# Transposing q and k of the last two units by transfers, fp32 dummy products and new orders in a fused linear-attention and max-out kernel

## The chip, the core and the metric

The kernel runs on one core of one Trainium2 chip. Times are device microseconds of one execution; the number of a kernel is the median of its runs.

## What is computed

The first half is a gated linear attention with a recurrent state of 48 x 48 for each of 4 batches and 8 heads, over 768 steps; its output, laid out as 3072 rows of 384, goes through a max-out layer (no bias) and an output product.

```python
for t in range(S):                                    # S = 768, D = 48, B = 4, H = 8
    state = alpha[:, :, t, :, None] * state + einsum('bhd,bhe->bhde', k[:, :, t], v[:, :, t])
    y[:, :, t] = einsum('bhd,bhde->bhe', q[:, :, t], state)
x = y.transpose(0, 2, 1, 3).reshape(3072, 384)
out = maximum(x @ w1, x @ w2) @ w_out                 # w1, w2: 384 x 1024, w_out: 1024 x 384
```

All inputs and the output are fp32. The kernel's products are in fp16, with sums in fp32.

## The kernel before, in words

The work is cut into 12 **units** of 256 rows (two chunks of 128 steps of one batch): unit u is batch u % 4, chunk pair u // 4. The layer is rewritten as max(x w1, x w2) w_out = relu(x (w1 - w2)) w_out + x (w2 w_out), so that each unit needs one product `h` against w1 - w2, a relu `g`, and a product `o` that adds the relu's share (`f` parts) and x's own share (`x` part).

Every step is an operation with a short name, which the orders below use. The number is the unit; units 0 and 1 are cut into two halves (.0, .1) for many steps.

- **Attention, up to the products.** `lg`, `ra`, `em`, `ep`, `de` (ScalarE: logarithm of alpha and exponentials), `sg` (sum of two steps' logarithms), `cs` (TensorE, L479 and L481: running sums of the logarithms), `k0`, `q0`, `kn`, `qn` (k and q times the decay factors, L414; `kn` on GpSimd or VectorE, `qn` on VectorE).
- **Transposes.** `tpq`, `tpk` (TensorE, L507): 16 transpositions each put q and k of a unit with the head's 48 channels along partitions, into two banks of PSUM; two copies `qk` (ScalarE or VectorE, L417) bring them to the tile QK in SBUF.
- **Attention products.** `pp` (L533, k against q, reads QK), `pt` (mask, VectorE, L545 and L550), `kv` (L582, new state), `tm`, `dd`, `sb` (state with its decay), `y` (L642: 112 or 88 small products from pt, v, QK and the state), `xt` (copy to fp16).
- **Layer.** `h` (L672, 6 products of 256 columns), `g` (L677 or L678), `o` (L699: an `f` part is two products, an `x` part three), `oc` (copy), `st` (store, issued from ScalarE's queue).
- **Weights, once.** `wt` (L382: w2 transposed in fp32, four transpositions a group, six groups), `wtc`, `woc` (to fp16), `w12` (w1 - w2 on VectorE, L398, four pieces), `wq` (L404: w2 w_out, 24 products), `wqc`.
- **Loads.** `ld.*`, all on SyncE's queue (L345 for alpha, q, k and v of the units, L367 for weights), 59 of them.

The program is written out by hand tables. ORDERS names, for each engine, every operation in the order in which the engine gets it. `Plan.follow` walks these tables with a planned duration for each operation. From the planned starts it takes two things: which of the eight banks of PSUM an operation gets, and where TensorE has gaps in the first 45 us. `Plan.gaps` lists the gaps, and `fill` puts **dummy products** of a tile of zeros (`wsrc`) there, sized so that they fill the gap. They keep TensorE running; nothing reads their result. An engine's instructions run in the order in which they stand, so a dummy that takes longer than its gap holds up what stands behind it. In `fill`, a gap that begins before 1.5 us counts double time.

Of the kernel before, what the change touches and what calls it, by code (L numbers as in the profile page):

```python
# [196 lines left out]
cs0.0 cs1.1 cs1.0 tpk0.0 cs0.1 tpq0.0 tpk1.1 pp0.0 tpk1.0 tpq1.1 kv1 tpq1.0 wt.20 pp1.0 tpq0.1 tpk0.1 kv0 pp1.1  # L197
wt.21 pp0.1 wt.10 wq.20 wq.21 wt.00 wt.01 y1.0 y1.1 y0.0 y0.1 wq.00 wq.22 wq.01 wq.10 wq.02 wq.23 wq.03 wq.11
wq.12 wt.11 wq.13 wq.24 wq.04 h0.0 wq.25 wq.05 h1.0 o0.0.f0 o0.1.f0 wq.14 wq.15 h1.1 h0.1 h0.2 wq.06 wq.26 wq.27
wq.16 wq.17 wq.07 cs2 o1.1.f0 o1.1.f1 o0.0.f1 h1.2 o0.1.f1 o0.1.f2 h0.3 cs3 o0.0.f2 o1.1.f2 h1.3 o0.0.f3 tpq2  # L200
tpk2 o0.1.f3 o0.1.x0 o1.1.f3 pp2 kv2 o1.1.x0 o0.0.x0 o1.0.f0 o1.0.f1 o1.0.f2 o1.0.f3 kv3 tpk3 tpq3 y2 o1.0.x0
cs4 h2.3 h2.0 h2.2 pp3 cs5 h2.1 o2.1.x0 o2.0.x0 o2.0.f0 o2.1.f0 tpq4 tpk4 y3 o2.1.f1 o2.0.f1 o2.0.f2 o2.1.f2
o2.0.f3 pp4 o2.1.f3 h3.3 h3.1 h3.0 o3.0.x0 kv4 tpq5 tpk5 kv5 cs6 h3.2 o3.0.f0 o3.0.f1 o3.1.x0 y4 o3.1.f0 o3.1.f1
o3.0.f2 o3.1.f2 o3.1.f3 pp5 h4.2 cs7 h4.1 o3.0.f3 h4.0 tpk6 kv6 tpq6 y5 o4.0.x0 o4.1.x0 o4.1.f0 h4.3 h5.0
o4.0.f0 h5.1 o4.1.f1 o4.0.f1 o4.1.f2 o4.1.f3 tpq7 tpk7 pp6 o4.0.f2 o5.1.x0 cs8 o4.0.f3 h5.2 h5.3 o5.1.f0 o5.1.f1
y6 kv7 tpk8 tpq8 o5.1.f2 o5.0.x0 o5.1.f3 o5.0.f0 o5.0.f1 pp7 o5.0.f2 cs9 h6.3 o5.0.f3 h6.0 h6.2 y7 pp8 tpk9 tpq9
h6.1 h7.3 h7.2 h7.1 o6.0.x0 o6.0.f0 h7.0 kv8 kv9 pp9 o6.1.x0 cs11 o7.1.x0 o6.0.f1 o7.1.f0 o6.0.f2 o7.1.f1
o6.1.f0 o6.1.f1 o7.1.f2 o6.1.f2 o6.1.f3 o6.0.f3 o7.0.x0 o7.0.f0 o7.0.f1 cs10 y8 y9 o7.0.f2 o7.0.f3 h8.3 h8.1
o7.1.f3 h8.2 h8.0 tpq11 kv11 tpk10 tpq10 tpk11 o9.1.x0 h9.0 h9.1 o9.0.x0 h9.2 kv10 pp10 o9.1.f0 o9.0.f0 h9.3
o9.1.f1 o9.0.f1 o9.0.f2 o9.1.f2 o8.0.x0 pp11 o8.1.x0 o8.0.f0 o8.1.f0 o9.0.f3 o8.1.f1 o8.1.f2 o8.0.f1 o8.0.f2 y10  # L210
y11 o8.0.f3 o9.1.f3 h10.0 h10.1 o10.1.x0 o10.0.x0 o10.0.f0 h11.2 h11.1 o11.0.x0 h11.0 o10.1.f0 h10.3 o11.1.x0
# [10 lines left out]
w6.01 w6.00 xt5.1 xt5.0 ep7 lg9 g4.3 g5.0 ra8 g5.1 oc4.1 w6.11 qk7.0 em8 de8 st2 ep8 g5.2 g5.3 lg10 oc4.0 xt6.1
qk8.0 ra9 oc5.1 xt6.0 em9 g6.3 ep9 oc5.0 de9 g6.0 g6.2 w9.10 st3 xt7.0 vc8 qk9.1 g6.1 st4 g7.3 lg11 st5 vc10
g7.0 w9.11 ra10 em11 de11 ep11 w10.01 ra11 w10.11 em10 xt8.0 xt8.1 de10 ep10 oc7.0 xt9.1 g8.1 w11.00 xt9.0
w10.00 g8.2 st6 w11.11 st7 qk10.0 qk11.0 g9.0 g9.1 g9.2 g9.3 xt10.0 xt11.0 g11.2 st9 g10.2 oc8.0 g10.3 oc8.1 st8
oc10.0 oc10.1 st10 st11.0 oc11.1 st11.1 st11.2
# [3 lines left out]
q00.0 qn0.0 kn1.1 q01.1 dm0 q01.0 k01.0 k00.1 qn1.1 qn1.0 qn0.1 pt0.0.1 qk1.0.1 pt0.0.0 tm1.0 pt1.0.0 qk0.1.0  # L230
tm0.0 pt1.1.1 pt1.1.0 pt1.0.1 pt0.1.1 pt0.1.0 tm0.1 xt1.1 zw2 xt0.0 w12.0 tm1.1 w12.1 wtc.11 g1.0 w12.2 g0.2
g0.1 w12.3 sg3 q02 qn2 k02 kn2 dm3 g1.3 qk2.1 qn3 k03 w2.00 tm2.0 pt2.0 pt2.1 tm3.0 qk3.1 xt2.1 qk3.0 tm3.1 g2.3
tm2.1 qn4 pt3.1 pt3.0 g2.1 qk4.0 qk4.1 k05 sg6 pt4.0 qn5 pt4.1 tm4.0 qk5.1 tm5.0 tm4.1 sb5.1 w5.00 k06 tm5.1 qn6
sg7 dm6 pt5.0 pt5.1 tm6.0 g4.0 dm7 vc7 k07 qk6.0 qk6.1 qn7 sb6.1 w7.11 tm6.1 qk7.1 pt6.1 pt6.0 qn8 kn8 w7.01
tm7.0 qk8.1 k09 pt7.1 pt7.0 tm7.1 qn9 xt7.1 dm9 pt8.1 pt8.0 qk9.0 g7.2 g7.1 sg11 tm8.0 tm9.0 sb9.1 pt9.0 pt9.1
q011 k010 oc6.1 oc6.0 q010 w9.01 kn10 k011 w11.01 qn10 qn11 oc7.1 sb11.0 g8.0 tm11.0 qk11.1 g8.3 qk10.1 tm10.0
w11.10 pt10.0 pt10.1 sb10.1 w10.10 pt11.0 pt11.1 xt10.1 oc9.0 g10.0 xt11.1 g10.1 g11.1 oc9.1 g11.0 g11.3 oc11.0
oc11.2
# [509 lines left out]
def kernel(  # L748
# [63 lines left out]
    def fill(t0, t1, b):  # L812
# [4 lines left out]
        while left > 0.06:  # L817
            cols = min(512, int(2400 * left / slow) - 5)
            nc.tensor.matmul(env["PB"][b][:, 0:cols], lhsT=w[:, 0:128], rhs=w[:, 0:cols], start=True, stop=True)  # L819
# [38 lines left out]
```

## Time and profile before

| | before |
|---|---|
| median of 3 runs (lowest, highest) | 133.82 us (133.79, 133.96) |
| profiled execution | 133.79 us, span 132.1 us |
| TensorE busy in the span | 124.8 us (95%), 2061 products |
| VectorE, ScalarE, GpSimd busy | 103.3, 95.4, 64.4 us |
| dummy products | 28, 9.4 us busy |
| loads and stores | 28.63 MB |

PE is TensorE's products, PEld its weight loads, DVE VectorE, ACT ScalarE, POOL GpSimd, SP SyncE; a q behind the name is the engine's queue, where transfers are issued. A row of the timeline is the start, the length, engine, line, operation, output and inputs, and how many such instructions follow each other. The length runs from the first start to the last end, and a product's end lies about 0.2 us behind the start of the next, since products are pipelined. A row of groups has count, busy time, mean of one in ns, and the idle time before them with what ended it. A row of a stretch has, for each engine, its busy time and its count. In the page's first line a TensorE that is busy may still be held up inside a product.

### The profile page before, as it was taken

Reading aid. Unit: us, or ns where it says so; the run is one execution under the profiler, and the core shown is the slowest. Engines: PE = TensorE matmul, PEld = TensorE weight load, DVE = VectorE, ACT = ScalarE, POOL = GpSimd, SP = SyncE. Lnnn points to the kernel's source line nnn. Section 1 sums busy time; section 2 is a strip of 40 time slices with the busy share of each in tenths; the row PEclk is TensorE's granted clock in tenths of the full one; section 3 lists DMA queues with packets and bytes.
Section 4 is the critical chain, followed back from the end, with each engine's and each line's share of the span. In section 5 each row is a group of like instructions: output and inputs, shape, how many; then the busy total and the mean of one; then the engine's idle time right before and its main releaser. Section 6 shows DMA issues by size and latency. Waiting matters only on the chain.

```text
span 132.1 us, 4911 instructions
## 1 busy us (share of the span) xinstructions
PE 124.8 (95%) x2061; PEld 88.9 (67%) x2061; DVE 103.3 (78%) x186; ACT 95.4 (72%) x198; POOL 64.4 (49%) x104
## 2 busy tenths in 40 slices
PE   6988889999999999999999999999999999999970
PEld 2444667777667766867776767976688765778650
DVE  5469997869999996998699969989988599355040
ACT  3688889568899999998996997998288920301540
POOL 6025970052759999958579399655146200000000
PEclk9999999999999999999999999999999999999999
DMA  3999999999999999999999999560003300002144
GB/s 89 325 325 363 415 371 342 341 297 260 252 302 311 280 261 293 322 334 251 318 314 270 300 275 285 193 241 5 0 5 122 121 0 0 5 0 90 69 181 144
DMA packets 56486, 28.63 MB, mean 217 GB/s; under 512 B 50320, under 2 KB 56080, under 8 KB 56464
## 3 DMA queue, kind: packets, MB, share of 16 engines
q1 hardware_dynamic: 53040, 23.60, 63.0%
q10 hardware_dynamic: 3424, 4.72, 9.9%
q8 instruction: 16, 0.26, 0.7%
q14 instruction: 6, 0.05, 0.1%
HBM read 23.59 MB, written 4.72 MB: 214 GB/s over the span
## 4 chain that ended last, share of the span: by engine, by line
PE 68%; SPq 7%; DVE 7%; DMA 6%; issue 4%; POOL 4%; DVEq 0%; POOLq 0%
PE pb L699 28%; PE pb L672 20%; PE pb L642 7%; SPq L345 6%; DMA w2f<-in_moe_w_dram 6%; PE pb L533 4%; PE pb L582 3%; PE pb L507 3%; PE pb L404 2%; SPq L367 2%; POOL kn L414 1%; DVE gt L677 1%; PE pb L382 1%; PE pb L479 1%; DVE w L417 1%
## 5 line engine op out<-in xcount | busy, mean ns | idle before, releaser
L699 PE MATMUL pb<-wo,gt 128*128 128x384 f16 (+2 forms) x200 | 37.5, 320 | 0.0
L672 PE MATMUL pb<-xt,w 128*128 128x256 f16 x288 | 36.5, 273 | 0.0
L672 PEld LDWEIGHTS <-w 128*128 128x128 f16 x288 | 27.6, 98 | 5.7
L678 ACT ACTIVATE gt<-pb 128x512 f16<-128x512 f32 x32 | 18.4, 600 | 11.5 <-PE pb L672 11.0
L545 DVE TENSOR_TENSOR pt<-pb,mask 128x1024 f16<-128x1024 f32 x20 | 23.6, 1217 | 2.5 <-PE pb L533 2.5
L699 PEld LDWEIGHTS <-gt 128*128 128x128 f16 x200 | 18.2, 98 | 9.9
L677 DVE TENSOR_SCALAR gt<-pb 128x512 f16<-128x512 f32 x16 | 10.9, 685 | 9.2 <-PE pb L672 8.8
L699 PE MATMUL pb<-w2o,xt 128*128 128x384 f16 (+2 forms) x75 | 15.2, 320 | 0.0
L417 ACT CAST xt<-pb 128x384 f16<-128x384 f32 x18 | 10.1, 592 | 5.6 <-PE pb L642 5.6
L414 POOL TENSOR_TENSOR sb<-tm,dd 128x384 f16<-128x384 f32 x15 | 12.9, 858 | 1.2 <-DVE tm L614 1.0
L614 DVE TENSOR_TENSOR tm<-pb,sb 128x384 f32<-128x384 f32 x16 | 8.6, 550 | 3.8 <-PE pb L582 3.5
L417 ACT COPY qk<-pb 128x1024 f16<-128x1024 f16 (+1 forms) x13 | 10.3, 818 | 1.6 <-PE pb L507 1.4
L417 ACT COPY os<-pb 128x384 f32<-128x384 f32 (+1 forms) x18 | 8.5, 473 | 3.9 <-PE pb L699 2.8
L819 PE MATMUL pb<-wsrc 128*128 128x512 f16 (+6 forms) x28 | 9.4, 480 | 1.3 <-DVE wsrc L825 1.3
L642 PE MATMUL pb<-pt,w 128*32 128x128 f16 x384 | 10.0, 220 | 0.0
L414 POOL TENSOR_TENSOR kn<-kf,em 128x768 f16<-128x768 f32 (+1 forms) x5 | 7.5, 1498 | 5.0 <-DVE kf L414 3.3
L417 DVE COPY qk<-pb 128x1024 f16<-128x1024 f16 (+1 forms) x15 | 9.5, 646 | 0.3
L414 POOL TENSOR_TENSOR qf<-qf,ra 128x384 f32<-128x384 f32 (+1 forms) x5 | 5.2, 1045 | 8.8 <-ACT pb L486 5.6
L484 ACT ACTIVATE em<-pb 128x384 f32<-128x384 f32 (+1 forms) x14 | 6.2, 442 | 4.5 <-PE pb L481 3.6
L642 PE MATMUL pb<-qk,sb 128*32 128x128 f16 x240 | 9.4, 219 | 0.0
L642 PEld LDWEIGHTS <-w 128*32 128x32 f16 x384 | 8.4, 96 | 1.5 <-issue 0.7
L699 PEld LDWEIGHTS <-xt 128*128 128x128 f16 x75 | 6.7, 98 | 3.5
(103 smaller groups left out, 232.1 us busy)
## 6 DMA issues: line engine op xcount, KB each, us to landing
out_dram<-os ACTq DMA_DIRECT2D x11, 384.0 KB, 3.0
af<-in_alpha_dram SPq DMA_DIRECT2D x8, 384.0 KB, 5.8
kf<-in_k_dram SPq DMA_DIRECT2D x8, 384.0 KB, 4.8
qf<-in_q_dram SPq DMA_DIRECT2D x8, 384.0 KB, 5.2
vf<-in_v_dram SPq DMA_DIRECT2D x8, 384.0 KB, 5.7
w2f<-in_moe_w_dram SPq DMA_DIRECT2D x3, 512.0 KB, 5.7
wof<-in_moe_w_out_dram SPq DMA_DIRECT2D x4, 384.0 KB, 8.6
w1f<-in_moe_w_dram SPq DMA_DIRECT2D x4, 384.0 KB, 9.8
```

The source lines that it names most:

```text
L345: nc.sync.dma_start(out=V(T_)[n].rearrange("p h r d -> p h (r d)"), in_=V(src)[b, :, t0 : t0 + 256, :].rearrange("h (p r) d -> p h (r d)", ...
L414: return lambda: getattr(nc, e).tensor_mul(out=o(), in0=x(), in1=y())
L417: return lambda: nc.scalar.copy(out=o(), in_=i()) if e == "scalar" else getattr(nc, e).tensor_copy(out=o(), in_=i())
L484: add(f"em{nq}", "ACT", lambda p=p, h_=h_: nc.scalar.activation(out=V("EM")[lg][:, h_], in_=csv(p), func=ACTF.Exp, scale=-1.0), 0.05 + 0.3 ...
L545: f = lambda e=e: nc.vector.tensor_mul(out=V("PT")[pt][:, e].rearrange("p a j x -> p (a j) x"), in0=pair(pp[e][0]).rearrange("p n (j x) -> ...
L614: nc.vector.tensor_add(out=V("TM")[new], in0=kvv, in1=V("SB")[m4])
L642: nc.tensor.matmul(o, lhsT=l, rhs=r, start=(a, qd) not in seen, stop=i == len(todo[qd]) - 1, skip_group_check=True)
L672: nc.tensor.matmul(t[:, m, :], lhsT=V("w12")[:, ds, f * 128 : f * 128 + 128], rhs=V("XT")[x3][:, ds, :], start=(ds == 0), stop=(ds == ND - 1))
L677: gd = lambda g2=g2, v2=v2: nc.vector.tensor_relu(out=g2(), in_=v2())
L678: ga = lambda g2=g2, v2=v2: nc.scalar.activation(out=g2(), in_=v2(), func=ACTF.Relu)
L699: nc.tensor.matmul(b32(x, w), lhsT=l, rhs=r, start=fst and y_ == 0, stop=lst and y_ == len(ws) - 1)
L819: nc.tensor.matmul(env["PB"][b][:, 0:cols], lhsT=w[:, 0:128], rhs=w[:, 0:cols], start=True, stop=True)
```

## The change

Four things change.

1. **q and k of units 10 and 11** are not transposed on TensorE any more. Eight transposing transfers on SyncE's queue (two each for q and k of each unit, 64 partitions x 1024 fp16 each), behind all loads, go from the tiles KN and QN straight into QK. The 64 transpositions and the four copies `qk` of these units go.
2. For that, `kn` and `qn` of these two units are written in another layout, each by two instructions of half the size, and `kv` of these units reads KN in that layout.
3. **Dummy products** read an fp32 `wsrc` instead of an fp16 one. `fill` and `fills` now reckon 1200 columns a microsecond where they had 2400.
4. All five **orders** are new, the loads' order too: the w1 loads come ahead of the second half of w_out, and w2.0 and w2.1 are the first weights. With new planned starts the banks of PSUM and the gaps for dummies differ too.

```diff
-                    count += 2 * self.fills(t - pe - 0.25)
+                    count += 2 * self.fills((t - pe - 0.25) / (2 if pe == 1.2 else 1))
...
     def fills(left):
-        return int(left / 0.215) + (left % 0.215 > 0.06)
+        return int(left / 0.43) + (left % 0.43 > 0.06)
...
     "SP": """
-ld.af0 ld.af1 ld.kf0 ld.kf1 ld.qf0 ld.qf1 ld.vf1 ld.vf0 ld.w2.2 ld.wo.0 ld.w2.1 ld.w2.0 ld.wo.1 ld.wo.2 ld.w1.0
...
+ld.af1 ld.af0 ld.kf0 ld.qf0 ld.qf1 ld.vf1 ld.kf1 ld.vf0 ld.w2.0 ld.w2.1 ld.wo.0 ld.wo.1 ld.w2.2 ld.w1.0 ld.w1.1
...
+TURN = (10, 11)
...
+            def kq(e, nm, src, fac, h_=h_):
+                def f():
+                    eng = getattr(nc, e)
+                    if u not in TURN:
+                        eng.tensor_mul(out=V(nm)[i3][:, :, h_, 0:D], in0=rhd(src())[:, :, h_], in1=bc(fac()))
+                        return
+                    o = V(nm)[i3].rearrange("p r h w -> p (r h w)").rearrange("p (j r e w) -> p r j e w", j=HP, r=2, e=2)
+                    for r in range(2):
+                        pe_ = lambda t: t.rearrange("p (j e) d -> p j e d", e=2)
+                        eng.tensor_mul(out=o[:, r, :, :, 0:D], in0=pe_(src()[:, :, r]), in1=pe_(fac()))
+                return f
...
-            for w, nm in enumerate(("qn", "kn")):
+            for w, nm in enumerate(("qn", "kn")) if u in TURN else ():
+
+                for a in range(2):
+                    add(f"ld.t{nm[0]}{u}.{a}", "SP", lambda w=w, nm=nm.upper(), a=a: nc.sync.dma_start(
+                        out=V("QK")[qk][:, a, w].rearrange("p j r c -> p (j r) c"),
+                        in_=V(nm)[i3][64 * a : 64 * a + 64].rearrange("p r h w -> p (r h w)"), transpose=True),
+                        1.25, reads=both(nm, i3), writes=[("qk", (qk, a), w)], key=P.nload, lat=1.9)
+                    P.nload += 1
+            for w, nm in enumerate(("qn", "kn")) if u not in TURN else ():
...
-            for a in range(2):
+            for a in range(2) if u not in TURN else ():
...
-    sbt("wsrc", [128, 512], FP16)
+    sbt("wsrc", [128, 512], FP32)
...
-            cols = min(512, int(2400 * left / slow) - 5)
+            cols = min(512, int(1200 * left / slow) - 5)
             nc.tensor.matmul(env["PB"][b][:, 0:cols], lhsT=w[:, 0:128], rhs=w[:, 0:cols], start=True, stop=True)
-            left -= (cols / 2400 + 0.002) * slow
+            left -= (cols / 1200 + 0.002) * slow
```

Three places of the orders matter below. The first is the head of TensorE's program. Before, the first batch of dummies ends like this, ahead of the first `cs` (tri and sg are its operands):

```order
L819 LDWEIGHTS wsrc_150
L819 MATMUL pb<-wsrc_150 128x512
L819 LDWEIGHTS wsrc_150
L819 MATMUL pb<-wsrc_150 128x479
L479 LDWEIGHTS tri_148
L479 MATMUL pb<-sg_83,tri_148 128x192
```

Now the program begins with six fp32 dummies; an fp32 product has no weight load of its own in this list:

```order
L840 MATMUL pb<-wsrc_150 128x512 x5
L840 MATMUL pb<-wsrc_150 128x477
L480 LDWEIGHTS tri_148
L480 MATMUL pb<-sg_84,tri_148 128x192
L482 LDWEIGHTS sg_84
L482 MATMUL pb<-ind_149,sg_84 128x4
```

And between the last `cs` and the first transposition (L527) stand six more:

```order
L482 LDWEIGHTS sg_83
L482 MATMUL pb<-ind_149,sg_83 128x4
L840 MATMUL pb<-wsrc_150 128x512 x5
L840 MATMUL pb<-wsrc_150 128x242
L527 LDWEIGHTS kn_89
L527 MATMUL pb<-ident_145,kn_89 128x64
```

Before, dummies stood between the `cs` as well; now all four `cs` stand together, with the two batches around them. Two smaller batches follow, of 384 columns ahead of the first `pp` and of 512 + 449 columns behind the second.

The second place is the end of SyncE's program. Before, it ends with the loads of units 10 and 11 (wof is the tile of w_out, used again for a unit's loads):

```order
L345 DMA wof_64<-in_v_dram 128x8x96
L345 DMA vf_79<-in_v_dram 128x8x96
L345 DMA wof_64<-in_k_dram 128x8x96
L345 DMA vf_80<-in_v_dram 128x8x96
L345 DMA wof_64<-in_q_dram 128x8x96
L345 DMA kf_72<-in_k_dram 128x8x96
L345 DMA qf_76<-in_q_dram 128x8x96
```

Now the transfers stand behind the last loads; qk_127 belongs to unit 10, qk_128 to unit 11:

```order
L346 DMA vf_80<-in_v_dram 128x8x96
L346 DMA wof_64<-in_v_dram 128x8x96
L515 DMA_TRANSPOSE qk_127<-kn_90 128x8x64
L515 DMA_TRANSPOSE qk_127<-qn_93 128x8x64 x2
L515 DMA_TRANSPOSE qk_127<-kn_90 128x8x64
L515 DMA_TRANSPOSE qk_128<-qn_94 128x8x64
L515 DMA_TRANSPOSE qk_128<-kn_91 128x8x64 x2
L515 DMA_TRANSPOSE qk_128<-qn_94 128x8x64
```

Unit 10's four transfers are issued first, then unit 11's four, and nothing is behind them.

The third place is VectorE's program where it makes q and k of unit 10 (kn_90, qn_93) and q of unit 11 (qn_94), after unit 9's `pt` (pt_129). Before:

```order
L545 TENSOR_TENSOR pt_129<-pb,mask_147 128x1024 x2
L414 TENSOR_TENSOR wof_64<-wof_64,ra_86 128x8x48
L414 TENSOR_TENSOR kf_72<-kf_72,af_68 128x8x48
L417 COPY os_138<-pb 128x384 x2
L414 TENSOR_TENSOR qf_76<-qf_76,ra_85 128x8x48
L417 CAST w_95<-vf_79 64x8x48
L414 TENSOR_TENSOR kn_90<-kf_72,em_87 128x16x48
L414 TENSOR_TENSOR wof_64<-wof_64 128x8x48
L417 CAST w_97<-wof_64 64x8x48
L414 TENSOR_TENSOR qn_93<-qf_76,pb 128x16x48
L414 TENSOR_TENSOR qn_94<-wof_64,pb 128x16x48
```

Now:

```order
L565 TENSOR_TENSOR pt_129<-pb,mask_147 128x1024 x2
L415 TENSOR_TENSOR qf_76<-qf_76,ra_85 128x8x48
L502 TENSOR_TENSOR kn_90<-kf_72,em_87 128x4x2x48 x2
L502 TENSOR_TENSOR qn_93<-qf_76,pb 128x4x2x48 x2
L418 CAST vc_99<-vf_80 128x768
L588 TENSOR_TENSOR de_103<-ex_114,own_113 128x32
L418 COPY os_138<-pb 128x384
L415 TENSOR_TENSOR wof_64<-wof_64,ra_86 128x8x48
L418 CAST xt_132<-pb 128x3x2x64
L502 TENSOR_TENSOR qn_94<-wof_64,pb 128x4x2x48 x2
```

k and q of unit 10 now follow unit 9's `pt` almost at once, each in two halves, and q of unit 11 comes after five other instructions. On TensorE `kv10`, `pp10`, `y10`, then `kv11`, `pp11` and later `y11` stand where units 8, 9 and 10 still have `h` and `o` products to do between them.

More of the change, by code (lines that the diff above doesn't have):

```diff
@@ L196 @@
     "PE": """
[L197 to L211, printed above, removed]
@@ L212 @@
-h10.2 o11.0.f0 o10.0.f1 o11.0.f1 o8.1.f3 o10.1.f1 o10.1.f2 o10.0.f2 h11.3 o10.0.f3 o11.1.f0 o11.0.f2 o10.1.f3
-o11.0.f3 o11.1.f1 o11.1.f2 o11.1.f3 o11.2.x0 o11.2.f0 o11.2.f1 o11.2.f2 o11.2.f3
+cs1.1 cs1.0 cs0.0 cs0.1 tpk0.0 tpq0.1 tpk0.1 tpq0.0 pp0.1 pp0.0 tpq1.1 tpk1.1 wt.01 kv0 pp1.1 wt.00 wt.10 tpk1.0
+tpq1.0 kv1 wt.11 pp1.0 y0.0 y0.1 wq.00 wq.10 wt.20 wq.11 wq.12 wq.01 wq.02 wq.03 wq.20 wq.21 wq.22 y1.0 y1.1
+h0.0 wt.21 wq.23 h1.0 h0.1 h1.1 h0.2 o0.0.f0 wq.13 h1.2 cs2 wq.24 o0.1.f0 wq.25 wq.04 wq.14 o0.0.f1 wq.15
@@ new lines @@
+o4.0.f0 o4.1.f0 o4.1.f1 o4.0.f1 o4.0.f2 h5.0 o4.0.f3 h5.1 pp6 tpk7 tpq7 o4.1.f2 o4.1.f3 o5.0.x0 h5.2 h5.3 y6 kv7
+tpq8 tpk8 o5.0.f0 o5.1.x0 h6.3 o5.0.f1 o5.0.f2 o5.1.f0 pp7 cs9 o5.1.f1 o5.1.f2 h6.0 o5.1.f3 o5.0.f3 h6.2 y7 pp8
+tpk9 tpq9 h6.1 h7.0 h7.1 o6.0.x0 o6.0.f0 kv8 kv9 pp9 o6.0.f1 cs10 o6.0.f2 h7.3 o6.1.x0 o6.0.f3 o6.1.f0 o7.0.x0
+o7.0.f0 o6.1.f1 y8 y9 o6.1.f2 h7.2 cs11 o7.1.x0 o6.1.f3 o7.0.f1 o7.0.f2 o7.1.f0 o7.0.f3 o7.1.f1 o7.1.f2 h8.1
+h8.2 o7.1.f3 h8.0 h9.3 o8.0.x0 o8.0.f0 o8.0.f1 h8.3 o8.0.f2 o8.1.x0 o8.1.f0 kv10 pp10 o8.0.f3 h9.2 o8.1.f1 h9.1
@@ L222 @@
[L222 to L226, printed above, removed]
+lg1.1 lg1.0 lg0.1 lg0.0 ra1.1 ra0.1 em1.1 em1.0 ra0.0 em0.0 em0.1 de1.0 de0.1 de0.0 ep1.1 ep0.0 ep1.0 de1.1
@@ L230 @@
[L230 to L238, printed above, removed]
+ind zsb0 zw0 zw1 zw2 zkn0 zsb1 zkn1 zqn2 zsg0 zsb2 own zsg1 sg1.1 trj zqn0 sg1.0 sg0.1 sg0.0 q00.1 k00.1 zqn1
+kn0.1 kn0.0 qn0.1 qn0.0 qk0.1.0 qk0.0.0 k01.1 k01.0 pt0.1.0 qn1.1 pt0.0.0 qk1.1.1 qn1.0 pt0.0.1 tm0.0 pt1.1.0
@@ L239 @@
+kn10 qn10 vc10 dm10 oc6.1 q011 xt9.0 qn11 g8.2 w11.01 g8.1 sb10.0 g8.3 tm10.0 pt10.0 pt10.1 g9.1 oc8.0 xt10.0
+sb11.0 xt10.1 pt11.1 oc8.1 pt11.0 tm11.0 sb11.1 g10.0 w11.10 xt11.0 g11.1 g11.2 oc10.0 oc10.1 oc11.2
 """,
     "POOL": """
-id16 id32 mask tri q00.1 kn1.0 dm1 dd0.1 vc0 w0.00 kn0.1 dd1.1 zsb3 woc.1 zsb1 sb1.1 w1.01 sb0.1 w1.11 woc.7 sg2
-dm2 dd2.1 q03 dd3.1 vc2 kn3 sb2.1 w3.01 sg4 sb3.1 sg5 q04 k04 dm4 kn4 q05 dd4.1 dm5 dd4.0 w4.11 dd5.0 sb4.0 kn5
-q06 sb5.0 w5.10 dd5.1 sb4.1 w5.11 kn6 sg8 dd6.0 vc6 sb6.0 q07 kn7 dd6.1 dd7.0 q08 k08 dd7.1 w6.10 sb7.0 sg9 sg10
@@ new lines, in gla @@
+            emf = lambda h_=h_: V("EM")[lg][:, h_]
+            two = 0.06 if u in TURN else 0.0
+            add(f"kn{nq}", "POOL", kq("gpsimd", "KN", KFn, emf), 0.2 + 1.6 / cut + 3 * two,
+                sh=True, reads=tk("kf", n, p) + tk("em", lg, p), writes=tk("kn", i3, p), key=q1("kn"),
+                alts={"DVE": (kq("vector", "KN", KFn, emf), 0.06 + 0.815 / cut + two)})
+            add(f"qn{nq}", "DVE", kq("vector", "QN", QFn, lambda p=p: csv(p)),
+                0.07 + 0.8 / cut + two, reads=tk("qf", n, p) + tk("csx", u, p) + [("dex", u, p)], writes=tk("qn", i3, p), ps=[cs[p]], key=q1("kn"))
```

55 lines of the change are left out of this document (35 added, 20 removed).

## Prediction

> **What bounds the kernel now.** I read the page first, then TensorE's busy time in stretches of the span, then TensorE's waits, then the chain that ended last, and at the end the timeline of the first 24 us. From the page, the stretches and the waits of TensorE from 19 us on:
>
> ```profile
> PE 124.8 (95%) x2061; PEld 88.9 (67%) x2061; DVE 103.3 (78%) x186; ACT 95.4 (72%) x198; POOL 64.4 (49%) x104
> 23.86:128.10 104.24, 104.04 (x1768) 76.71 (x1766) 84.55 (x125) 76.58 (x153) 53.65 (x75) 1.00 0.68 194
> PE pb L382 <- DMA w2f<-in_moe_w_dram: 0.4, 1, 0.4
> ```
>
> From 23.86 us, where the first `h` product (h0.0) starts, TensorE is busy in 104.04 of 104.24 us, and its only listed wait after 19 us is 0.4 us for a weight load. VectorE (84.55) and ScalarE (76.58) have room in the same stretch. So the end is the start of h0.0 plus the products that are then left. The chain, then the timeline of TensorE:
>
> ```profile
> 11.11 7.76 DMA w2f<-in_moe_w_dram
> 21.53 1.57 PE pb L404 x9
> 26.63 1.98 PE pb L672 x18
> 125.26 2.80 PE pb L699 x27
> 1.25 4.85 PE L819 MATMUL pb<-wsrc 128*128 128x512 f16 x11 [1.25 <-DVE wsrc L825]
> 5.89 0.37 PE L479 MATMUL pb<-sg,tri 128*128 128x192 f16 x1
> 6.15 0.88 PE L819 MATMUL pb<-wsrc 128*128 128x512 f16 x2
> 7.22 0.97 PE L819 MATMUL pb<-wsrc 128*128 128x512 f16 x4
> 23.86 0.82 PE L672 MATMUL pb<-xt,w 128*128 128x256 f16 x6
> ```
>
> The dummies (L819) fill the start. Products stop at 128.06 us; the last copy and store behind them are not touched. So there are two questions: how much product work the change takes from those 104.2 us, and when h0.0 can start.
>
> **The work left at h0.0.** The rows for what leaves and for what moves across h0.0:
>
> ```profile
> 34.60 0.41 PE L507 MATMUL pb<-ident,qn 64*128 64x64 f16 x16
> 34.84 0.40 PE L507 MATMUL pb<-ident,kn 64*128 64x64 f16 x16
> L382 PE MATMUL pb<-ident,w2f x24: 272/273/330, 14.1 to 23.3; 128*128 128x128 f32 x24
> 19.00 1.06 PE L382 MATMUL pb<-ident,w2f 128*128 128x128 f32 x8 [0.44 <-DMA w2f<-in_moe_w_dram]
> ```
>
> A group of 16 transpositions takes 0.24 us (34.60 to 34.84). Four groups go (tpq and tpk of units 10 and 11): 0.96 us. I add 0.1 us for one turn fewer between kinds of product in the new list: 1.05 us less in all. But the new list has done less when it comes to h0.0: 10 `wq` products instead of 14 (1.57 over 9, 0.17 each) and 5 groups of `wt` instead of 6 (eight transpositions of w2f in 1.06 us, less the last one's own 0.27, over seven: 0.11 each, 0.45 a group of four). That puts 1.1 us back. So about 104.3 us are left at h0.0 in both kernels, and the difference in time is the difference in h0.0's start. The four copies `qk` out of PSUM that go too (two on ScalarE, two on VectorE) were beside TensorE's work: nothing.
>
> **The dummies.** In fp16 and warm a column costs 1.98 us over 18 x 256, 0.43 ns. At the start it is twice that: the first eleven dummies hold 10 x 512 + 479 = 5599 columns and take 4.64 us (1.25 to 5.89), 0.83 ns. The rate changes between the dummies of 6.15 and those of 7.22 us; I take 7.1. In fp32 the trace has only the transpositions of w2f, 0.11 us for 128 columns: 0.86 ns, twice fp16. That is one pass. The built program holds one weight load and one product for each of those, but two of each for every fp32 dummy; a plain fp32 product is not in the trace. So a dummy's column costs between 0.86 ns (if both passes together cost what this one does) and 1.72 ns (if each does). I take 1.72, since the two are the same kind of instruction as the measured one. `fill` sizes them at 1200 columns a us, 0.83 ns: by my value each batch runs twice as long as its gap.
>
> The Trainium skill's FP8 and Floating Point Precision page (TensorE Precision Notes) says that a true fp32 product takes four passes through the array; four times 0.43 would be 1.72 ns too, and no run here shows it yet.
>
> The memset ahead of the first batch:
>
> ```profile
> 0.92 0.27 DVE L825 MEMSET wsrc<- 128x256 uint32 x1 [0.92 <-PEq L842]
> ```
>
> The new list has 15 dummies in four batches: 5 x 512 + 477 = 3037 columns ahead of cs1.1; 5 x 512 + 242 = 2802 ahead of tpk0.0; 384; 961. The first starts at 1.5 us (1.25, and 0.27 more for twice the words). Up to 7.1 us it gets through 5.6 / 0.00344 = 1630 columns, the other 1407 take 2.4 us: end at 9.5, where the old `cs` stood at 5.89. Four `cs` halves, 0.13 us each (half of 5.89 to 6.15): 10.05. The second batch, 2802 x 1.72 ns = 4.8 us: 14.85. Meanwhile ScalarE and VectorE need, from 10.05 on, by these rows:
>
> ```profile
> L484 ACT ACTIVATE em<-pb 128x192 f32<-128x192 f32 x4 | 1.3, 323 | 0.3 <-PE pb L481 0.3
> L486 ACT ACTIVATE pb<-pb 128x192 f32<-128x192 f32 x4 | 1.3, 331 | 0.0
> L488 ACT ACTIVATE ex<-pb 128x8 f32<-128x8 f32 x4 | 0.7, 172 | 0.3 <-PE pb L481 0.3
> L464 ACT ACTIVATE ra<-lg 128x192 f32<-128x192 f16 x4 | 1.4, 348 | 0.0
> L414 DVE TENSOR_TENSOR qn<-qf,pb 128x384 f16<-128x384 f32 x4 | 2.0, 547 | 0.1
> ```
>
> 1.3 + 1.3 + 0.7, one of the fourth (0.35) and one `qn` (0.5): 14.2. So kn and qn are ready before the dummies let the transpositions through. These, four halves of 0.12 and a turn, end at 15.4.
>
> **From there to h0.0.** VectorE's list from the first transpositions to w12.0, which h0.0 reads, has these beside `qn`:
>
> ```profile
> L550 DVE TENSOR_TENSOR pt<-pb,mask 128x512 f16<-128x512 f32 x8 | 5.1, 682 | 0.0
> L417 DVE COPY qk<-pb 128x512 f16<-128x512 f16 x2 | 0.8, 418 | 0.1
> L414 DVE TENSOR_TENSOR kf<-kf,af 128x192 f32<-128x192 f32 x4 | 1.3, 352 | 0.2 <-DMA kf<-in_k_dram 0.2
> L616 DVE COPY tm<-pb 128x384 f32<-128x384 f32 x4 | 2.2, 548 | 0.0
> L398 DVE TENSOR_TENSOR w<-w1f,w2f 128x768 f16<-128x768 f32 x4 | 3.8, 950 | 0.2 <-DMA w1f<-in_moe_w_dram 0.2
> 22.27 0.96 DVE L398 TENSOR_TENSOR w<-w1f,w2f 128x768 f16<-128x768 f32 x1 [0.15 <-DMA w1f<-in_moe_w_dram]
> ```
>
> Eight pt 5.1, four qk 1.6, two qn 1.0, two kf 0.65, two tm 1.1, one small memset 0.15 (half of 0.27), one w12 0.95: 10.6 us. So w12.0 ends at 26.0 and h0.0 starts at 26.1. TensorE's own items there (the last two batches, 2.3 us; wt 2.2; wq 1.7; the small products of units 0 and 1) fit beside it. In before, w12.0 waited for its load (last row) and h0.0 stood at 23.86. The new load order brings w1.0 one load sooner, but after this delay nothing waits for a load, so that gain is covered. h0.0 is 2.25 us later, the end 2.3: 134.4 us of span. The profiled execution took 133.79 us with a span of 132.1 (the median is 133.82), so 136.1.
>
> **The transposing transfers.** They replace products, if they land in time. Rows for what TensorE has to do meanwhile, for VectorE, and for the bounds:
>
> ```profile
> 78.71 0.55 PE pb L533 x16
> 79.69 0.16 PE pb L479
> 79.86 0.08 PE pb L481 x4
> 90.42 4.90 PE pb L699 x30
> 95.56 1.68 PE pb L642 x112
> L545 DVE TENSOR_TENSOR pt<-pb,mask 128x1024 f16<-128x1024 f32 x20 | 23.6, 1217 | 2.5 <-PE pb L533 2.5
> L414 DVE TENSOR_TENSOR kn<-kf,em 128x384 f16<-128x384 f32 x2 | 1.1, 553 | 0.0
> 10.12 0.43 SPq L367 DMA_DIRECT2D wof<-in_moe_w_out_dram  x1
> 17.32 4.26 SPq L367 DMA_DIRECT2D wof<-in_moe_w_out_dram  x1
> 79.02 1.39 SPq L345 DMA_DIRECT2D qf<-in_q_dram  x1
> out_dram<-os ACTq DMA_DIRECT2D x1, 128.0 KB, 2.0
> ```
>
> After pp9 VectorE has two pt (2.35), q0 (0.55, as large as half a kn), kn10 and qn10 in two halves each (2.2): the first transfer can go 5.1 us after pp9. The loads are then over (last issue 79.02) and nothing else is queued on SP. From pp9 to kv10 TensorE has pp9 (0.55), two cs (0.5), 53 products of `o` (4.90 over 30: 8.7), seven `h` (0.66 each: 4.6) and two `y` (1.7): 16 us; and 4.5 more to pp11. With t from one issue to the next and 2.0 us from issue to landing (the 128 KB store, the same size), pp10 waits if 5.1 + 4t + 2 is over 16, pp11 if 5.1 + 8t + 2 is over 20.5: from t = 1.7. The rows bound t between 0.43 and 4.26; I take 1.4, the last ordinary load's issue: no wait. The halves of kn and qn cost VectorE a few tenths, beside TensorE.
>
> **Rivals.** One: *the fp32 dummies take what `fill` plans* (0.86 ns). Then the first batch ends at 6.7 and the second before 10; 3.65 us of ScalarE and one qn after `cs` (7.25) give the transpositions at 11.4, and VectorE's 10.6 us from 11.8 give w12.0 at 22.3, when w1.0 has landed too. h0.0 at 22.4, 1.45 us sooner than before: 132.4. Against it speaks the pass of 0.11 us; for it, that the fp32 weight load may be what holds that row, and that columns alone cost less. Chance 0.16.
>
> Two: *the transfers are late*. The price is 8 us for each us of t above 1.7: at 3 us, 10 us more, near 146. For it, the 4.26 us issue; against it, that this one was issued while the loads ahead of it filled the queue. Chance 0.06. The Trainium skill's VectorE: DVE Perf Modes page (The three transpose paths) gives 1309 ns for 128x128 by DMA; as an estimate from that page, the four such areas of one transfer, one after the other, make t 5.2 us and the end 28 us later. No run here shows it.
>
> The forecast (two passes a dummy, transfers in time) has 0.78.
>
> **Numbers.** The forecast is 136.1. If the clock comes 2 us sooner, the first batch ends 1 us sooner, and the durations summed above overlap at their ends by up to 1 us in all: 134.0. If VectorE waits for ScalarE's qk copies (1 us) and the new order has waits of its own (0.9 us): 138.0. That holds the forecast's 0.78 and a little of the late transfers. The three runs of before spread by 0.13%, so 0.2% is about what can be told from no change. Faster 0.16 (rival one), same 0.02 (the foot of the forecast), slower 0.82.
>
> **What would show it.** In the profile after: two rows of products for each dummy, a warm pass of 512 columns near 0.44 us; `cs` from 9.5 us; the first transpositions at 15; h0.0 at 26; TensorE dense after it; pp10 and pp11 without a wait for a DMA. The prediction is wrong if h0.0 starts before 24 us, or if pp10 or pp11 waits for the transfers.

## The result, and the profile after

The changed kernel takes 135.58 us (median of 4 runs, 135.12 to 136.34) against 133.82 us (133.79 to 133.96): a ratio of 1.0135, 95% interval 1.0087 to 1.0183. The profiled execution took 135.12 us with a span of 133.4 us. Further down, the ratios leave out executions that are over 1.5% slower than their kernel's fastest (the medians do not), and the profiled executions with the second batch halved, with the late batches halved and with the transpositions placed anew are among these, so only the places of single steps are read from them.

Busy time and the group of the dummies on the page:

```profile
PE 128.4 (96%) x1999; PEld 90.5 (68%) x1999; DVE 101.0 (76%) x185; ACT 91.2 (68%) x189; POOL 67.9 (51%) x114
L840 PE MATMUL pb<-wsrc 128*128 128x512 f32 (+4 forms) x30 | 14.9, 644 | 1.5 <-DVE ind L300 1.5
```

TensorE has 62 products fewer and is busy 3.6 us longer. The 15 dummies are 30 rows of products, two for each, 14.9 us against 9.4 before. The stretch from the first `h` product to the last product:

```profile
26.29:130.02 103.73, 103.71 (x1715) 76.57 (x1711) 82.83 (x127) 73.52 (x147) 56.08 (x83) 1.00 0.74 199
```

From h0.0 on TensorE is dense, as before. Its timeline up to there, and its last row:

```profile
1.52 7.18 PE L840 MATMUL pb<-wsrc 128*128 128x512 f32 x12 [1.52 <-DVE ind L300]
8.53 0.25 PE L480 MATMUL pb<-sg,tri 128*128 128x192 f16 x1
9.07 4.95 PE L840 MATMUL pb<-wsrc 128*128 128x512 f32 x12
13.95 0.29 PE L527 MATMUL pb<-ident,kn 64*128 64x64 f16 x8
26.29 0.83 PE L693 MATMUL pb<-xt,w 128*128 128x256 f16 x6
129.39 0.61 PE L720 MATMUL pb<-wo,gt 128*128 128x128 f16 x8
```

The first `cs` (L480) stands at 8.53 where it stood at 5.89, the first transposition (L527) at 13.95, h0.0 at 26.29 where it stood at 23.86. From h0.0 to the last product's end it is 103.71 us (26.29 to 130.00), before 104.20. The transfers, by their source line:

```profile
L515 SPq DMA_TRANSPOSE qk<-kn x4: 1221/1263/1287, 96.4 to 105.0; - x4
L515 SPq DMA_TRANSPOSE qk<-qn x4: 1200/1242/1814, 97.8 to 106.3; - x4
DMA to landing us min/median/max: 2.6/2.7/3.8
107.02 0.23 PE L553 MATMUL pb<-qk 48*128 48x128 f16 x1
111.85 0.23 PE L553 MATMUL pb<-qk 48*128 48x128 f16 x1
```

Eight issues from 96.4 to 106.3 us are 1.41 us from one to the next. Unit 10's last transfer lands at 103.7, and pp10, its reader, starts at 107.02; unit 11's last lands at 109.0 (106.3 and 2.7), and pp11 starts at 111.85. TensorE's list of waits has one row, the start:

```profile
PE pb L840 <- DVE ind L300: 1.5, 1, 1.5
```

### The profile page after: what moved, and what is told of

It reads as the page before. It is cut to its first block, busy times and chain, and to the rows that moved or that the text cites. A ratio compares the mean times of both kernels' runs of the same rounds, so it can differ in the third digit from the quotient of the medians.

```text
span 133.4 us, 4799 instructions
## 1 busy us (share of the span) xinstructions
PE 128.4 (96%) x1999; PEld 90.5 (68%) x1999; DVE 101.0 (76%) x185; ACT 91.2 (68%) x189; POOL 67.9 (51%) x114
## 4 chain that ended last, share of the span: by engine, by line
PE 93%; DVE 3%; issue 1%; ACT 0%; ACTq 0%
PE pb L720 32%; PE pb L693 24%; PE pb L840 11%; PE pb L663 8%; PE pb L553 5%; PE pb L527 4%; PE pb L405 3%; PE pb L602 3%; PE pb L480 2%; DVE pt L570 1%; PE pb L383 1%; PE pb L482 1%; DVE tm L637 0%; ACT os L418 0%; DVE wsrc L846 0%
## 5 line engine op out<-in xcount | busy, mean ns | idle before, releaser
L720 PE MATMUL pb<-wo,gt 128*128 128x384 f16 (+2 forms) x200 | 39.3, 320 | 0.0
L698 DVE TENSOR_SCALAR gt<-pb 128x512 f16<-128x512 f32 x17 | 11.6, 686 | 7.9 <-PE pb L693 7.8
L840 PE MATMUL pb<-wsrc 128*128 128x512 f32 (+4 forms) x30 | 14.9, 644 | 1.5 <-DVE ind L300 1.5
L418 DVE COPY qk<-pb 128x1024 f16<-128x1024 f16 (+1 forms) x14 | 8.4, 608 | 4.2 <-PE pb L527 4.2
L840 PEld LDWEIGHTS pb<-wsrc 128*128 128x128 f32 x30 | 6.1, 214 | 8.0 <-issue 6.4
L418 ACT COPY qk<-pb 128x1024 f16<-128x1024 f16 (+1 forms) x10 | 8.4, 846 | 3.4 <-PE pb L527 3.4
L663 PE MATMUL pb<-pt,w 128*32 128x128 f16 x384 | 10.4, 220 | 0.0
L663 PEld LDWEIGHTS <-w 128*32 128x32 f16 x384 | 8.5, 96 | 2.7 <-issue 2.0
L418 ACT CAST w<-vf 64x384 f16<-64x384 f32 x19 | 9.7, 509 | 0.3
L418 ACT COPY os<-pb 128x384 f32<-128x384 f32 (+1 forms) x15 | 7.1, 470 | 4.0 <-DVE os L418 2.7
L663 PE MATMUL pb<-qk,sb 128*32 128x128 f16 x240 | 9.7, 219 | 0.0
```

The costliest lines, as they stand in the source:

```text
L418: return lambda: nc.scalar.copy(out=o(), in_=i()) if e == "scalar" else getattr(nc, e).tensor_copy(out=o(), in_=i())
L663: nc.tensor.matmul(o, lhsT=l, rhs=r, start=(a, qd) not in seen, stop=i == len(todo[qd]) - 1, skip_group_check=True)
L698: gd = lambda g2=g2, v2=v2: nc.vector.tensor_relu(out=g2(), in_=v2())
L720: nc.tensor.matmul(b32(x, w), lhsT=l, rhs=r, start=fst and y_ == 0, stop=lst and y_ == len(ws) - 1)
```

## The experiments

The theory: the fp32 dummies take twice the time that `fill` plans for them, that puts h0.0 later, and transfers and orders cost nothing. The rivals: the new orders or the transfers cost the time; the type itself does harm; or the transfers are worth nothing. All ratios are against the kernel before on the same chip.

| kernel | median us | ratio to before (95%) | first cs | first transposition | h0.0 |
|---|---|---|---|---|---|
| changed | 135.58 | 1.0135 (1.0087, 1.0183) | 8.53 | 13.95 | 26.29 |
| changed, fp16 dummies | 132.39 | 0.9869 (0.9832, 0.9905) | 5.50 | 10.62 | 23.09 |
| changed, half the fp32 columns | 132.33 | 0.9882 (0.9843, 0.9921) | 6.04 | 10.71 | 23.18 |
| changed, no dummies | 132.94 | 0.9903 (0.9868, 0.9938) | 5.63 | 10.30 | 24.49 |
| before, fp32 dummies | 137.79 | 1.0265 (1.0224, 1.0306) | 8.82 | 11.83 | 28.21 |
| changed, first batch halved | 134.61 | 1.0057 (1.0037, 1.0076) | 6.36 | 11.83 | 25.20 |
| changed, second batch halved | 134.59 | 1.0036 (1.0011, 1.0062) | 9.50 | 12.57 | 26.54 |
| changed, late batches halved | 134.85 | 1.0065 (1.0028, 1.0102) | 9.53 | 14.94 | 26.59 |
| fp16 dummies, transpositions back | 135.25 | 1.0061 (1.0034, 1.0087) | 6.14 | 10.53 | 23.48 |
| the same, placed anew | 134.10 | 1.0000 (0.9974, 1.0025) | 6.02 | 10.68 | 23.68 |
| before, transfers alone | 134.76 | 1.0055 (1.0039, 1.0072) | 5.89 | 7.76 | 24.41 |
| changed, each transfer twice | 152.24 | 1.1375 (1.1354, 1.1397) | 8.47 | 13.88 | 26.23 |

**The dummies' type.** In the changed kernel:

```diff
-    sbt("wsrc", [128, 512], FP32)
+    sbt("wsrc", [128, 512], FP16)
...
-            cols = min(512, int(1200 * left / slow) - 5)
+            cols = min(512, int(2400 * left / slow) - 5)
...
-            left -= (cols / 1200 + 0.002) * slow
+            left -= (cols / 2400 + 0.002) * slow
```

> The changed kernel with fp16 dummies at 2400 columns a us again, all else as changed. If the doubled time of the fp32 dummies is what delayed h0.0: the first cs at about 6.3 us, h0.0 at 22.4 instead of 26.29, TensorE dense behind it, and with the 103.2 us that were left at h0.0 in the changed kernel a time of 131.2 us; 132.4 if the small waits of the kernel before come back with the earlier start. If the new orders or the transfers are what costs, the time stays near 135.5.

Measured 132.39 us (131.63 to 133.0), 3.2 us under the changed kernel and 1.3% under before. TensorE in its profile:

```profile
1.25 4.35 PE L840 MATMUL pb<-wsrc 128*128 128x512 f16 x12 [1.25 <-DVE ind L300]
10.62 0.29 PE L527 MATMUL pb<-ident,kn 64*128 64x64 f16 x8 [1.09 <-DVE kn L497]
23.09 0.83 PE L693 MATMUL pb<-xt,w 128*128 128x256 f16 x6
75.45 0.28 PE L527 MATMUL pb<-ident,kn 64*128 64x64 f16 x8
76.67 0.29 PE L527 MATMUL pb<-ident,kn 64*128 64x64 f16 x8 [0.94 <-issue]
```

h0.0 is 3.2 us sooner, and the median is 3.2 us lower, so the dummies carry the whole loss. It is not the 3.9 us expected: 23.09, not 22.4 (why, below). The last two rows are a wait of another kind, met again below.

**The same columns' time in fp32.** The type stays, the columns are halved:

```diff
-            cols = min(512, int(1200 * left / slow) - 5)
+            cols = min(512, int(600 * left / slow) - 5)
...
-            left -= (cols / 1200 + 0.002) * slow
+            left -= (cols / 600 + 0.002) * slow
```

> The changed kernel with its fp32 dummies reckoned at 600 columns a us, so that each batch has half the columns (1519 in the first, 1402 in the second). If only the time of the batches matters and not the type, this is like the fp16 dummies: first cs at 6.5 to 6.8 us, h0.0 near 22.5, 131.2 to 132.4 us. If fp32 products harm in another way (the clock, the stretch behind them), it stays above 134.

Measured 132.33 us (131.92 to 133.26), the same as with fp16:

```profile
1.52 4.69 PE L840 MATMUL pb<-wsrc 128*128 128x512 f32 x6 [1.52 <-DVE ind L300]
7.08 2.60 PE L840 MATMUL pb<-wsrc 128*128 128x512 f32 x6
23.18 0.83 PE L693 MATMUL pb<-xt,w 128*128 128x256 f16 x6
```

So the type does no harm, only the time of the batches. This version and the one with fp16 beat both kernels.

**fp32 dummies in the kernel before.** The edit of the first experiment the other way round, in the kernel before.

> The kernel before with fp32 dummies at 1200 columns a us (2809 columns ahead of the first cs, 6775 in all), orders and transposes untouched. If a fp32 column costs 1.72 ns warm and twice that before the clock comes, the first batch ends at 8.6 to 9.1 us where cs stood at 5.89: 2.7 to 3.2 us later, and a little more from the batches behind it: 136.3 to 137.8 us. If the type is not to blame: 133.8, no change.

Measured 137.79 us (137.12 to 138.32), at the top of what was expected:

```profile
1.52 7.47 PE L819 MATMUL pb<-wsrc 128*128 128x512 f32 x12 [1.52 <-DVE wsrc L825]
8.82 0.25 PE L479 MATMUL pb<-sg,tri 128*128 128x192 f16 x1
28.21 0.49 PE L672 MATMUL pb<-xt,w 128*128 128x256 f16 x3
```

The first `cs` is 2.9 us later, h0.0 4.35 us; the batches behind `cs` brought the other 1.4. The fp32 dummies cost 3.9 us with the old orders (137.79 less 133.92) and 3.2 with the new.

**One batch at a time.** A rate of 600 for the gaps that begin before 1.5 us; from 1.5 to 9; and after 9:

```diff
+        rate = 600 if t0 < 1.5 else 1200
...
-            cols = min(512, int(1200 * left / slow) - 5)
+            cols = min(512, int(rate * left / slow) - 5)
...
-            left -= (cols / 1200 + 0.002) * slow
+            left -= (cols / rate + 0.002) * slow
```

> The changed kernel with half the columns in the first batch of fp32 dummies only. The cs end at 7.1 as with all batches halved, the second batch takes 4.9 us, the first transposition starts at 12.0 instead of 13.95, h0.0 at 24.3: 133.6 us. If the first batch alone is to blame: 132.3. If it is not on the path at all: 135.6.

> The changed kernel with half the columns in the second batch of fp32 dummies only. The first cs stands at 8.5 as in the changed kernel, the second batch ends at 11.5, kn and qn of both halves are ready by 12.3, so that the transpositions run from 11.5 to 12.7 and h0.0 stands at 24.0 to 24.3: 133.3 to 133.6 us. If the second batch alone is to blame: 132.3. If the chain on ScalarE and VectorE hides it: 135.6.

> The changed kernel with half the columns in the third and fourth batch of fp32 dummies only (those around the first pp). The prediction had h0.0 wait for VectorE's list, with TensorE's own work fitting beside it: then h0.0 stays within 0.3 us of 26.3. If TensorE's own products are the bound from the first transposition to h0.0 (12.3 us without an idle stretch), the two batches give back 1.0 to 1.3 us: h0.0 at 25.0 to 25.3, 134.3 to 134.6 us.

Measured 134.61 (134.04 to 135.09), 134.59 (133.25 to 135.77) and 134.85 us (134.25 to 136.62): each about 1 us under the changed kernel, none the 2 us hoped for with the first two, and the third a little over its 134.3 to 134.6. No batch is to blame alone. Two things that the expectations did not have stand in the profiles. First, TensorE waits for no data, for 1 to 2 us. With the first batch halved:

```profile
PE pb L527 <- issue: 0.9, 1, 0.9
PE pb L663 <- issue: 0.8, 1, 0.8
```

With the second:

```profile
PE pb L663 <- issue: 1.1, 1, 1.1
```

The L663 waits stand ahead of h0.0. Without the first of them h0.0 would be at 24.4 (25.20 less 0.8), as expected. Second, the clock. In the stretches from 5 to 7 and from 7 to 9 us TensorE (the first count) runs 6 and 15 products in the changed kernel:

```profile
5.00:7.00 2.00, 2.00 (x6) 0.95 (x5) 1.28 (x8) 1.65 (x5) 0.21 (x1) 1.00 1.17 325
7.00:9.00 2.00, 2.00 (x15) 1.01 (x14) 0.77 (x3) 0.16 (x1) 0.38 (x1) 1.00 1.17 325
```

With the late batches halved, where the same first batch runs, 4 and 6; the third row is the stretch from the first transposition to h0.0:

```profile
5.00:7.00 2.00, 2.00 (x4) 0.87 (x3) 1.24 (x8) 1.60 (x5) 0.28 (x1) 1.00 1.17 326
7.00:9.00 2.00, 2.00 (x6) 0.90 (x5) 0.77 (x3) 0.00 (x0) 0.32 (x1) 1.00 1.17 324
14.94:26.59 11.65, 11.42 (x251) 7.98 (x251) 10.97 (x22) 10.30 (x21) 7.16 (x14) 1.00 1.09 363
```

A pass of 512 columns takes 0.85 us before the clock comes and 0.43 behind it. In the changed kernel's profile it came at 5.2 us, in this one and the second batch's at 7.2: `cs` at 8.53 and at 9.5, with the same program up to there. These are also the times at which each trace's records of the granted clock begin; ahead of its first record a row of a stretch has nothing to go by and reads 1.00, so the 1.00 in these rows does not mean full speed. With the second batch halved, h0.0 at 26.54 less 1.0 for the clock and 1.1 for the wait is 24.4, close to what was expected. With the late batches halved, the stretch from the first transposition to h0.0 took 11.65 us against 12.34: 0.7 back, not the 1.0 to 1.3 expected, but not the 0 of a bound on VectorE.

**No dummies at all.**

```diff
-    todo += [(t0 + 1e-4, -1, lambda g=(t0, t1, b): fill(*g)) for t0, t1, b in P.gaps(45.0, 0.25)]
+    todo += [(t0 + 1e-4, -1, lambda g=(t0, t1, b): fill(*g)) for t0, t1, b in P.gaps(45.0, 0.25)[:0]]
```

> The changed kernel without any dummy products. If they serve only to be in the way, h0.0 stands where the halved batches let it stand (23.2) or a little sooner: 132.0 to 132.4. If they are what gets TensorE its full clock by 7 us: the cs and the transpositions still start at about 6 and 10.7 (they wait for their operands), but the clock stays at half until some 5 us of dense work have gone by behind 12 us, so that 5 to 8 us of work take twice as long: 135 to 140.

Measured 132.94 us (132.17 to 133.28): 2.6 us faster than with the change's dummies, and not to be told from the well-sized ones (132.33, overlapping intervals). The expected 135 to 140 is wrong, though the half clock that it rested on is there. TensorE's timeline:

```profile
10.30 0.40 PE L527 MATMUL pb<-ident,kn 64*128 64x64 f16 x8 [2.88 <-DVE kn L497]
16.58 1.97 PE L383 MATMUL pb<-ident,w2f 128*128 128x128 f32 x8
18.48 0.40 PE L527 MATMUL pb<-ident,kn 64*128 64x64 f16 x8
24.49 0.28 PE L693 MATMUL pb<-xt,w 128*128 128x256 f16 x1
```

Eight fp32 transpositions take 1.97 us where a warm group takes 1.06, so the clock is at half until about 19 us (the clock records begin at 19.6). But TensorE is busy for only 7.7 us between 10.3 and 19, partly in the place of waits, and h0.0 is just 1.3 us later than with well-sized dummies.

**The transfers in the old orders.** The kernel before with the change's parts 1 and 2; tpq, tpk and qk of units 10 and 11 are struck from its lists, and the transfers stand behind its loads:

```diff
 ld.kf8 ld.kf9 ... ld.qf11 ld.kf10 ld.qf10
+ld.tk10.0 ld.tk10.1 ld.tq10.0 ld.tq10.1 ld.tk11.0 ld.tk11.1 ld.tq11.0 ld.tq11.1
```

> The kernel before, its orders, loads and fp16 dummies as they are, but with q and k of units 10 and 11 by the eight transposing transfers behind the loads (the layout of kn, qn and kv that goes with them too), in the order k then q of unit 10, k then q of unit 11. With 1.25 us from issue to issue and 2.7 us to landing, as the changed kernel shows, and kn10 ready at 97.1 us: unit 10 has landed at 103.6, a us ahead of pp10 (104.6), unit 11 at 108.6, 0.2 us behind pp11's place (108.4). So 0.96 us of products go and 0.2 come back: about 133.0 to 133.2. If the transfers are worth nothing without the new orders: 133.9 or more.

Measured 134.76 us (five executions from 134.25 to 134.94, one at 178.05): 0.55% slower than before, a miss. TensorE's waits for the transfers:

```profile
PE pb L554 <- DMA qk<-qn: 1.6, 2, 0.8
```

And SyncE's issues, two to a row:

```profile
97.86 3.21 SPq L516 DMA_TRANSPOSE qk<-kn  x2
101.58 2.88 SPq L516 DMA_TRANSPOSE qk<-qn  x2
104.64 2.52 SPq L516 DMA_TRANSPOSE qk<-kn  x2
107.26 2.53 SPq L516 DMA_TRANSPOSE qk<-qn  x2
```

The expectation took an issue's own 1.25 us for the time from issue to issue. From the first issue to the eighth, at 108.56, it is 10.7 us, 1.53 each. So unit 10 landed at 106.4, not 103.6, and unit 11 at 111.2, not 108.6; both `pp` waited. Without orders that bring kn and qn early, the transfers give back more (1.6 us of waits) than they save (0.96 us of products). In this execution h0.0 is 0.55 us later too, and what part of the loss that is stays open.

**Each transfer twice.** A second, equal `dma_start` behind each of the eight.

> The changed kernel with each of the eight transposing transfers issued twice, one behind the other, from the same tile to the same place. If the queue takes 1.25 us for each and 2.7 us go from issue to landing: unit 10's last lands at 107.9 (first issue 96.4, seven more, 2.7), 0.8 us behind pp10's start; unit 11's last at 117.9, 5.1 us behind where pp11 then stands: 5.9 us in all, 141.5. If a transfer costs the queue much less than its spacing shows, or several run side by side: near 135.6.

Measured 152.24 us. TensorE's waits:

```profile
PE pb L558 <- DMA qk<-qn: 6.7, 1, 6.7
PE pb L558 <- DMA qk<-kn: 5.3, 1, 5.3
```

Two stretches behind such waits (the figure behind the five engines is the granted clock):

```profile
110.00:115.00 5.00, 2.30 (x16) 1.44 (x17) 1.59 (x2) 0.00 (x0) 0.00 (x0) 0.59 0.31 52
125.00:130.00 5.00, 3.47 (x24) 2.00 (x25) 2.39 (x3) 0.00 (x0) 0.00 (x0) 0.50 0.15 25
```

`pp` waits for the last landing, as the sum has it, but 12 us instead of 5.9: five of the second transfers are listed as waiting, 5.3 us in all, until the first one to the same place had landed, so it is 27.5 us from the first of 16 issues to the last (96.26 to 123.78), 1.83 each. And the waits cost more than themselves: during each the granted clock fell to 0.5 and stayed there for 6.8 us (from 110.9 and from 124.6 by the clock records), and six `h` products took 1.48 us there against 0.82.

**The transpositions back on TensorE,** in the changed kernel with fp16 dummies, in two placements:

```diff
-TURN = (10, 11)
+TURN = ()
...
-h8.2 o7.1.f3 h8.0 h9.3 o8.0.x0 o8.0.f0 ...
+h8.2 o7.1.f3 h8.0 tpk10 tpq10 h9.3 o8.0.x0 o8.0.f0 ...
```

The order shown is that of the first placement.

> The changed kernel with fp16 dummies and with the 64 transpositions and four copies of units 10 and 11 back on TensorE, ScalarE and VectorE, no transposing transfers. If the transfers replace 0.96 us of products at no other cost, this is 0.96 to 1.05 us slower than the same kernel with transfers (about 132.3 if that has 131.2). If the transfers cost time somewhere (a wait of pp10 or pp11, or slower loads), it is as fast or faster.

> The changed kernel with fp16 dummies and with the transpositions of units 10 and 11 on TensorE again, as tried before, but placed anew: they and their copies, and some 40 of the steps around them, stand elsewhere in the lists, so that pp11 finds its bank free. If the transfers are worth the 0.96 us of products and the turns between kinds, 0.95 to 1.3 us slower than with transfers: 133.3 to 133.7, about the time of the kernel before. If what the first try lost (2.9 us) belongs to the transpositions themselves: 134.8 or more.

The first, 135.25 us (134.28 to 138.98), is 2.6 us slower than with transfers by the two ratios. In its profile the first transposition waits 1.1 us, and pp11 0.8 us for a bank:

```profile
PE pb L526 <- DVE kn L496: 1.1, 1, 1.1
PE pb L552 <- DVE xt L417: 0.8, 1, 0.8
```

And behind the first of these waits the granted clock falls to 0.70 and 0.50:

```profile
12.00:14.00 2.00, 1.97 (x21) 0.91 (x20) 2.00 (x6) 1.97 (x6) 1.38 (x3) 0.70 1.06 427
14.00:16.00 2.00, 2.00 (x22) 1.17 (x20) 1.09 (x3) 1.55 (x3) 2.00 (x4) 0.50 1.02 393
```

The second, 134.10 us (133.12 to 135.68), is 1.7 us slower than with transfers, 1.2 to 2.3 by the two intervals (their half widths added in squares): more than the 0.96 us of products, and it meets the expected 0.95 to 1.3 only at its foot. The transfers are worth at least what they take from TensorE. What the rest is, the copies and the banks or the waits for no data (1.4 us in its profile), the spread does not let me tell. Its profile has half clock too, from 12.6 to 16.0 us by the clock records; that is not the rest, since the executions whose mean granted clock is above 0.99 differ by the same 1.7 us (medians of 134.06 and 132.35). Without the transfers the new orders, with fp16 dummies, take the old kernel's time (ratio 1.0000).

## Why the prediction was right

**The end is h0.0 plus the work left.** Held. Of the 2.4 us by which h0.0 moved (23.86 to 26.29), 1.3 reached the span. The terms behind h0.0 were off: the prediction had 0.05 us more work left than before, the runs show 0.5 less (103.71 against 104.20), and from the last product's end to the end of the span 3.4 us against 4.0, where it said that nothing was touched. Together some 1.2 us; less the 0.2 us by which h0.0 came later than forecast, that is the difference between the span of 134.4 forecast and 133.4.

**A dummy is two passes of fp32.** Right: two rows for each, 0.43 us a pass of 512 columns warm, 1.68 ns a column in all against 1.72 taken. By the Trainium skill's FP8 and Floating Point Precision page (TensorE Precision Notes) it would be four passes; the trace has two of half speed, which is the same time.

**The batches.** Right in size, and off by the clock. The prediction let it come at 7.1 us, and `cs` at 9.5. It came at 5.2 in the profile after, at 7.2 in two others, which have `cs` at 9.5. The range had a term for it, and it was the right one: 2 us of clock for 1 us of time. The first transposition stood at 13.95 instead of 14.85 for that reason alone.

**From there to h0.0.** This step failed, though its number came out: "VectorE's list", 10.6 us, was to put w12.0 at 26.0 and h0.0 at 26.1, with TensorE's items fitting beside it. VectorE in the profile after:

```profile
14.50 0.76 DVE L418 COPY qk<-pb 128x512 f16<-128x512 f16 x2 [2.19 <-PE pb L527]
18.26 0.42 DVE L418 COPY qk<-pb 128x512 f16<-128x512 f16 x1 [0.71 <-PE pb L527]
23.99 0.95 DVE L399 TENSOR_TENSOR w<-w1f,w2f 128x768 f16<-128x768 f32 x1
```

w12.0 was done at 24.9, 1.35 us ahead of h0.0, and VectorE waited 0.7 us for TensorE on the way. With that wait its list took about the time forecast (10.4 us, from 14.5 on), but h0.0 did not wait for its end. TensorE's own stretch from the first transposition to h0.0 is this:

```profile
13.95:26.29 12.34, 12.26 (x253) 8.23 (x253) 11.06 (x22) 10.49 (x21) 7.17 (x14) 1.00 1.08 367
```

Busy in 12.26 of 12.34 us: TensorE is the bound. The prediction summed 6.2 us of its products (dummies, wt, wq), which by the starts of their groups took 7.1, and left the small products of units 0 and 1 unsummed; they are the other 5.2. That the stretch begins 0.9 us sooner and is 1.1 us longer than the prediction had it made the number good by chance. With well-sized dummies h0.0 falls to 23.1 and not to 22.4 for a like reason. In the kernel with fp16 dummies:

```profile
20.34 0.63 PE L383 MATMUL pb<-ident,w2f 128*128 128x128 f32 x4 [0.28 <-DVE pt L570]
21.46 0.96 DVE L399 TENSOR_TENSOR w<-w1f,w2f 128x768 f16<-128x768 f32 x1 [1.21 <-DMA w1f<-in_moe_w_dram]
```

w12.0 waits for its load again and is done at 22.4, but TensorE, which waits for VectorE's `pt` until 20.34, has 2.75 us of products from there to h0.0. VectorE has no listed wait between 9 us and that `pt`, so there both lists bind, one after the other.

**The transfers.** Right: 1.41 us from issue to issue (1.4 taken), 2.7 us to landing (2.0 taken), and no wait, with 3.3 us to spare at pp10 and 2.8 at pp11, where the prediction's own sum gives 3.3 and 2.2. The prediction's estimate from the Trainium skill's VectorE: DVE Perf Modes page (The three transpose paths), four times 1309 ns and so 5.2 us an issue, does not agree with the trace's 1.41 us for this shape. That this sum decides is shown by the transfers in the old orders, which came too late by it.

**The rivals.** The first fell: the fp32 dummies take twice what is planned. But its time, 132.4 us for dummies that fit, is what the two kernels with such dummies measured, 132.39 and 132.33, with h0.0 0.7 us later than it said and less left behind it. The second fell with the transfers' times.

So the account of the change, from measured medians: fp32 dummies of twice the planned time +3.2 us (135.58 less 132.39); transfers and new orders together -1.5 us against the kernel before on the same chip (132.39 less 133.92).

## What to carry to other kernels

Filler that stands in an engine's order is work like any other: when its type or size changes, measure how long one piece takes, and check what happens with none at all before tuning it. To see which engine sets a step, sum every engine's own list over that stretch, the one with room included. A transfer that replaces products pays only if its operands are made early enough: count from the first issue with the time from issue to issue, not with an issue's own length.
